# Products with v, of the whole rows and of the next scores stand in one run on TensorE

## The chip, the cores and the metric

The kernel runs on one core of one Trainium2 chip. Its time is the device time of one execution in microseconds (us); the median of three executions before the change is 774.03 us (773.8 to 777.21).

## What is computed

Block-sparse attention, and behind it a feed-forward block without a bias. Batch 4, 8 heads, 768 positions, 64 values per head, blocks of 32 positions (24 blocks):

```
scores = scale * np.matmul(q, k.transpose(0, 1, 3, 2))
mask = |blk_i - blk_j| <= 1, or blk_i or blk_j is the first or the last block,
       or blk_j is one of 3 sampled blocks of blk_i
attn = softmax of scores where mask holds
attn_out = np.matmul(attn, v)
x = attn_out as 3072 tokens x 512
h = np.maximum(x @ w_in, 0.0)        # 512 x 2048
return (h * h @ w_out)               # 2048 x 512
```

Rows of the first and the last block see all keys (the whole rows); every other row sees two edge blocks, three sampled ones and a window of three.

## The kernel before, in words

**Feed-forward part.** The 3072 tokens go in 8 chunks of 384 (`UC` = 3 tiles of 128). `moe(c)` first turns the chunk's x on TensorE (tiles xt), and then, for each of 16 slices f of the hidden layer, issues `project(c, f - 2)` and `hidden(c, f)`. Both split fp32 into a high and a low fp32r part: `hidden` is 12 matmuls of 384 columns into one PSUM bank ph (L754), `project` three groups of 3 matmuls of 512 columns into po_0 to po_2 (L792). Between them ScalarE writes r (L758) and gh (L765), VectorE gf (L770) and the high parts of the weights (L720), GpSimd the low parts (L721, L772).

**Attention part.** The work of the 24 tiles of 128 rows is done in halves of 4 heads: class `Half`, 48 in all. A half does its scores s (64 small matmuls counted as the trace counts them, 64 rows by 32 columns of the array each, L365), maxima and the subtraction on VectorE (L376, L382), 16 exponentials on ScalarE that write straight into turned blocks (L404), a transposition on VectorE (pT, L409), products with v (pv: 64 small matmuls of 128 rows by 32 columns, L450) and the division by the sum on VectorE (`norm`, L465 to L470). After `norm` it loads the v of the next tile's same half: `loads(2)`, 1 or more window loads and 12 sampled ones on SP's queue (L297, L310), into the only buffer that there is for it. Class `Whole` does two heads of a batch's whole rows (4 units a batch): scores g (L528), maxima, exponentials pg, transpositions ptg on TensorE, copies pTg, products with v (pvg: 48 small matmuls, L570) and `norm` (L581 to L589). The unit with pr = 1 loads the batch's second vn behind its products (L215), into the buffer that they read.

**What sets the order.** Each engine runs its instructions in the order in which the program issues them. `moe(c)` is a generator that yields after every third of `hidden` and every group of `project`: six yields for each f, 96 a chunk. At every yield `Stream.step` first resumes the running units whose time has come, in the order in which they began, and then begins new ones. Halves begin every `STEP` = 16 yields, wholes of an even chunk `STEP // 2` = 8 yields behind their half. Inside a unit, `yield lag[...]` says how many yields later it goes on, at least one. With `LAG`, a half's products come 31 yields after its scores, one before the scores of the next half but one; a whole's come 15 yields after its beginning, 23 after the half that it stands beside. `LAG_1` is used for the units of chunk 1, `LAG_0` for those of chunk 0; these units run in their older form, with transpositions on TensorE where `moved` is false.

**Buffers.** s, g, pt, ptg, pv, pvg, xt and ph share 5 PSUM banks (pool `ps`, tag "s"). p, pm and pg share 3 buffers, pT and pTg 2.

## Time and profile before

| | us |
|---|---|
| median of three executions | 774.03 |
| lowest, highest | 773.8, 777.21 |
| the profiled execution | 776.91 |
| its span, first to last instruction | 775.1 |
| PE busy | 748.6 (97%) |
| ACT busy | 498.7 (64%) |
| DVE busy | 494.2 (64%) |
| POOL busy | 474.8 (61%) |

PE is TensorE, DVE VectorE, ACT ScalarE, POOL GpSimd, SP the engine that issues most transfers. In a timeline a row is a run of equal instructions: its start, how long it lasts from the first start to the last end, engine, line, what it writes and reads, and the count; "[... <-X]" would say that the engine stood idle before it, and for what. The time that a run takes of the engine is the distance from its start to the start of the next row, since matmuls overlap at their ends. The trace counts every small fp32 matmul twice (64 for the 32 of a pv).

### The profile page before, as it was taken

The numbers are of one execution on the slowest core, as the hardware profiler recorded it, in microseconds if no ns is written. First come the engines' busy times: TensorE is split into PE (matmuls) and PEld (weight loads), VectorE is DVE, ScalarE is ACT, GpSimd is POOL, SyncE is SP. The second block draws the span as 40 slices with busy tenths as digits, with TensorE's granted clock in tenths as the row PEclk, the third lists the DMA queues.
The fourth block names the chain that finished last, engine by engine and source line by source line (L and its number), as shares of the span: only waits on it lengthen the run. The fifth ranks groups of instructions, "written<-read, shape, count | busy, mean of one in ns | idle before, by whom it ended". The sixth has DMA issues, their size and how long they took to land.

```text
span 775.1 us, 26234 instructions
## 1 busy us (share of the span) xinstructions
PE 748.6 (97%) x9904; PEld 618.2 (80%) x9904; DVE 494.2 (64%) x1005; ACT 498.7 (64%) x1079; POOL 474.8 (61%) x552
## 2 busy tenths in 40 slices
PE   6679998999999999999999999999999999999997
PEld 3556676668888888888888888888888888888996
DVE  5996785657675666667666576667766565644442
ACT  2487877787666776776767767767666685733222
POOL 6993843215567476645556566754556665776885
PEclk9899999999999999999999999999999999999999
DMA  8766789545323535645324343644423342201001
GB/s 277 215 175 207 223 273 329 149 107 164 102 59 100 147 89 151 182 114 147 108 74 110 92 124 104 222 116 140 116 75 98 86 137 74 54 2 42 0 1 41
DMA packets 92289, 97.45 MB, mean 126 GB/s; under 512 B 14787, under 2 KB 79428, under 8 KB 92164
## 3 DMA queue, kind: packets, MB, share of 16 engines
q1 hardware_dynamic: 86036, 72.41, 34.0%
q0 software_dynamic: 5696, 22.58, 8.5%
q8 instruction: 79, 1.29, 0.7%
q10 hardware_dynamic: 432, 0.79, 0.3%
q14 instruction: 46, 0.38, 0.2%
HBM read 89.43 MB, written 6.29 MB: 123 GB/s over the span
## 4 chain that ended last, share of the span: by engine, by line
PE 88%; DVE 4%; DMA 4%; SPq 1%; ACT 1%; issue 1%; ACTq 0%; POOL 0%; POOLq 0%
PE ph L754 34%; PE po L792 31%; PE s L365 6%; PE pv L450 6%; PE po L782 3%; PE g L528 3%; DMA V<-in_v_dram 3%; PE pvg L570 2%; PE xt L739 1%; PE ptg L550 1%; DVE m L376 1%; DVE V L210 1%; DMA KG<-in_k_dram 1%; PE pt L428 1%; DMA kn<-in_kn_dram 1%
## 5 line engine op out<-in xcount | busy, mean ns | idle before, releaser
L404 ACT ACTIVATE pm<-p 32x256 f32<-32x256 f32 x576 | 239.0, 415 | 14.1 <-DVE p L382 5.8
L754 PE MATMUL ph<-xh,wi 128*128 128x384 f32 x832 | 238.9, 348 | 0.0
L792 PE MATMUL po<-wo,gh 128*128 128x512 f32 x672 | 216.1, 403 | 0.0
L772 POOL TENSOR_TENSOR gl<-gf,gh 128x384 fp32r<-128x384 f32 x112 | 115.9, 1035 | 126.3 <-DVE gf L770 110.8
L721 POOL TENSOR_TENSOR wi<-W,wi 128x512 fp32r<-128x512 f32 x104 | 143.4, 1378 | 78.0 <-DVE wi L720 46.4
L758 ACT ACTIVATE r<-ph 128x384 f32<-128x384 f32 x128 | 62.9, 492 | 199.0 <-PE ph L754 198.7
L721 POOL TENSOR_TENSOR wo<-WO,wo 128x512 fp32r<-128x512 f32 x112 | 145.7, 1301 | 56.5 <-DVE wo L720 55.4
L770 DVE SCALAR_TENSOR_TENSOR gf<-ph,r 128x384 f32<-128x384 f32 x112 | 62.3, 557 | 178.1 <-ACT r L758 163.4
L754 PEld LDWEIGHTS ph<-xh,wi 128*128 128x128 f32 x832 | 151.8, 189 | 12.2 <-issue 8.4
L754 PE MATMUL ph<-xl,wi 128*128 128x384 f32 x416 | 143.0, 344 | 0.0
L792 PEld LDWEIGHTS po<-wo,gh 128*128 128x128 f32 x672 | 121.7, 188 | 23.7 <-issue 2.8
L792 PE MATMUL po<-wo,gl 128*128 128x512 f32 x336 | 133.1, 396 | 0.0
L720 DVE CAST wo<-WO 128x512 fp32r<-128x512 f32 x112 | 87.9, 785 | 0.2
L754 PEld LDWEIGHTS ph<-xl,wi 128*128 128x128 f32 x416 | 78.6, 189 | 8.1 <-issue 2.6
L792 PEld LDWEIGHTS po<-wo,gl 128*128 128x128 f32 x336 | 63.2, 188 | 15.5 <-POOL gl L772 0.6
L376 DVE TENSOR_REDUCE m<-s 128x2 f32<-128x512 f32 x96 | 61.7, 684 | 18.0 <-PE s L365 17.6
L765 ACT ACTIVATE gh<-r 128x384 fp32r<-128x384 f32 x112 | 58.9, 526 | 10.1
L450 PEld LDWEIGHTS pv<-V,pT 128*32 128x32 f32 x3072 | 48.0, 109 | 19.7 <-issue 9.2
L450 PE MATMUL pv<-V,pT 128*32 128x65 f32 x3072 | 56.6, 221 | 6.4 <-DMA V<-in_v_dram 2.4
L754 PE MATMUL ph<-xh,WI 128*128 128x384 f32 x192 | 55.2, 348 | 0.8 <-ACT xh L742 0.8
L365 PE MATMUL s<-KG,q 64*32 64x160 f32 x1536 | 50.2, 304 | 0.9 <-issue 0.7
L409 DVE STREAM_TRANSPOSE pT<-pm 128x1024 f32<-128x1024 f32 x36 | 44.6, 1239 | 5.0 <-ACT pm L404 5.0
(81 smaller groups left out, 870.6 us busy)
## 6 DMA issues: line engine op xcount, KB each, us to landing
craw<-in_w_dram POOLq DMA_DIRECT2D x32, 512.0 KB, 5.6
V<-in_v_dram SPq DMA_DIRECT2D x504, 32.5 KB, 1.7
KG<-in_k_dram SPq DMA_DIRECT2D x216, 64.0 KB, 1.9
V<-in_v_dram SPq DMA_DIRECT2D x28, 390.0 KB, 4.1
q<-in_q_dram SPq DMA_DIRECT2D x24, 256.0 KB, 2.9
out_dram<-ot SPq DMA_DIRECT2D x21, 256.0 KB, 2.7
V<-in_v_dram SPq DMA_DIRECT2D x16, 292.5 KB, 4.1
vn<-in_vn_dram SPq DMA_DIRECT2D x5, 780.0 KB, 5.8
```

What stands on the lines that cost most here:

```text
L365: nc.tensor.matmul(self.sb[e][j * BLK : (j + 1) * BLK, i * NSLOT + a : i * NSLOT + z], q[r, j, pr, :], k, start=True, stop=True,)
L376: nc.vector.tensor_reduce(m[:, e], self.sb[e].rearrange("p (i c) -> p i c", i=2), axis=AX, op=ALU.max)
L404: nc.scalar.activation(p[a * BLK : (a + 1) * BLK, j], x[j * BLK : (j + 1) * BLK, :, a], AF.Exp, scale=SCALE)
L450: nc.tensor.matmul(po[j * BLK : (j + 1) * BLK, h * VW : (h + 1) * VW], self.pT[:, j, 2 * e + i, c], v[:, self.u, j, hv : hv + VW], start=( ...
L720: nc.vector.tensor_copy(w[:, 0], src)
L721: nc.gpsimd.tensor_tensor(w[:, 1], src, w[:, 0], op=ALU.subtract)
L754: nc.tensor.matmul(ph[:, :TOK], w, x, start=(i == 0), stop=(i == len(steps) - 1))
L758: nc.scalar.activation(r, ph[:, :TOK], AF.Relu)
L765: nc.scalar.activation(gh, r, AF.Square)
L770: nc.vector.scalar_tensor_tensor(gf, ph[:, :TOK], 0.0, r, op0=ALU.max, op1=ALU.mult)
L772: nc.gpsimd.tensor_tensor(gl, gf, gh, op=ALU.subtract)
L792: nc.tensor.matmul(acc[c][u], g[:, at], w[:, k], start=(f == 0 and i == 0), stop=(f == NF - 1 and i == 2))
```

## The change

The numbers in `LAG` are new, a second test lets `norm` follow its products at once, and the wholes begin 9 yields behind a half in place of 8. A half's products now come 32 yields after its scores and a whole's 32 after those of its half: at the same yield as the scores of the next half but one, and in front of them, since running units are resumed before new ones begin. `LAG_1` sets the old values back for chunk 1.

```diff
-LAG = {"s": 0, "e": 4, "v": 10, "x": 4, "t": 4, "c": 0, "v0": 5, "n": 0}
+LAG = {"s": 0, "e": 4, "v": 11, "x": 4, "t": 4, "c": 0, "v0": 13, "n": -1}
+
+G_AT = 9
 
-LAG_1 = {**LAG, "x": 3, "t": 6}
+LAG_1 = {**LAG, "v": 10, "x": 3, "t": 6, "v0": 5, "n": 0}
...
             po = self.values(bank)
-            yield lag["n"]
+            if lag["n"] >= 0:
+                yield lag["n"]
             self.norm(po)
...
-        both += [(at + i * STEP + STEP // 2, u) for i, u in enumerate(wholes)]
+        both += [(at + i * STEP + G_AT, u) for i, u in enumerate(wholes)]
```

On TensorE, in batch 1 (names are name, batch, tile or pair of heads, half): pv1_0_1 are the products of half 1 of tile 0, pvg1_1 those of the second whole, s1_1_1 the scores two halves on. Before:

```order
L754 MATMUL ph1_2_3424<-xh1_3147,wi1_2_3353 128x384 x2
L570 MATMUL pvg1_1_3429<-vn1_0_2394,pTg1_1_3384 32x65 x24
L754 MATMUL ph1_2_3424<-xl1_3148,wi1_2_3353 128x384
...
L754 MATMUL ph1_3_3506<-xh1_3147,wi1_3_3400 128x384
L450 MATMUL pv1_0_1_3533<-V0_75,pT1_0_1_3413 32x65 x4
...
L792 MATMUL po1_0_3403<-wo1_2_3421,gh1_2_3479 128x512 x2
L792 MATMUL po1_0_3403<-wo1_2_3421,gl1_2_3483 128x512
L365 MATMUL s1_1_1_0_3617<-kn1_1_2598,q1_1_2600 32x96
...
L792 MATMUL po1_1_3404<-wo1_2_3421,gh1_2_3479 128x512 x2
```

And now:

```order
L758 MATMUL ph1_3_3472<-xh1_3122,wi1_3_3400 128x384
L796 MATMUL po1_0_3403<-wo1_2_3421,gh1_2_3441 128x512 x2
L796 MATMUL po1_0_3403<-wo1_2_3421,gl1_2_3445 128x512
L453 MATMUL pv1_0_1_3506<-V0_75,pT1_0_1_3413 32x65 x4
...
L574 MATMUL pvg1_1_3582<-vn1_0_2394,pTg1_1_3397 32x65 x24
L368 MATMUL s1_1_1_0_3617<-kn1_1_2598,q1_1_2600 32x96
...
L796 MATMUL po1_1_3404<-wo1_2_3421,gh1_2_3441 128x512 x2
```

The three small runs, which large matmuls parted, stand together between two groups of `project`. Behind the opening stage, 34 runs of pv are followed by s at once, or by pvg and then s (12 of the 34); before none of them was. The two last halves have no later scores and stand alone as before.

On VectorE, at the same place (rec and recg are the reciprocals in `norm` of a half and of a whole, m the maxima of the scores). Before:

```order
L581 TENSOR_SCALAR recg1_1_3461<-pvg1_1_3429 128x1
L582 RECIPROCAL recg1_1_3461<-recg1_1_3461 128x1
L589 TENSOR_TENSOR x1_0_3174<-pvg1_1_3429,recg1_1_3461 32x64 x2
...
L770 SCALAR_TENSOR_TENSOR gf1_3_3529<-ph1_3_3506,r1_3_3525 128x384
L720 CAST wi1_5_3567<-W15_83 128x512
L465 TENSOR_SCALAR rec1_0_1_3573<-pv1_0_1_3533 128x4
...
L376 TENSOR_REDUCE m1_1_1_3702<-s1_1_1_0_3617 128x2
```

And now:

```order
L774 SCALAR_TENSOR_TENSOR gf1_3_3495<-ph1_3_3472,r1_3_3491 128x384
L724 CAST wi1_5_3500<-W15_83 128x512
L468 TENSOR_SCALAR rec1_0_1_3539<-pv1_0_1_3506 128x4
...
L585 TENSOR_SCALAR recg1_1_3609<-pvg1_1_3582 128x1
L586 RECIPROCAL recg1_1_3609<-recg1_1_3609 128x1
L593 TENSOR_TENSOR x1_0_3241<-pvg1_1_3582,recg1_1_3609 32x64 x2
...
L379 TENSOR_REDUCE m1_1_1_3694<-s1_1_1_0_3617 128x2
```

Both divisions now stand in front of the maxima of the new scores; before, the whole's stood one slice of the hidden layer earlier. On SP's queue the load of the second vn of batches 1 to 3 moves behind the 13 loads of v that follow the half's products; before it stood in front of them.

## Rows read from the trace of the kernel before

**Rows 1.** The page: busy time of TensorE; the chain that ended last.

```profile
PE 748.6 (97%) x9904; PEld 618.2 (80%) x9904; DVE 494.2 (64%) x1005; ACT 498.7 (64%) x1079; POOL 474.8 (61%) x552
...
PE 88%; DVE 4%; DMA 4%; SPq 1%; ACT 1%; issue 1%; ACTq 0%; POOL 0%; POOLq 0%
```

**Rows 2.** Busy time by stretch: length, each engine (instructions), clock, DMA share, GB/s.

```profile
257.00:345.00 88.00, 88.00 (x1185) 75.44 (x1185) 56.73 (x106) 63.54 (x143) 56.07 (x47) 1.00 0.50 139
```

**Rows 3.** Timeline of TensorE, 305 to 315 us: start, length, instruction.

```profile
305.81 1.12 PE L450 MATMUL pv<-V,pT 128*32 128x65 f32 x64
306.86 0.73 PE L792 MATMUL po<-wo,gh 128*128 128x512 f32 x2
...
307.75 0.40 PE L365 MATMUL s<-kn,q 64*32 64x96 f32 x16
...
308.89 0.44 PE L754 MATMUL ph<-xh,wi 128*128 128x384 f32 x1
...
311.08 0.62 PE L792 MATMUL po<-wo,gh 128*128 128x512 f32 x2
...
313.18 0.34 PE L754 MATMUL ph<-xh,wi 128*128 128x384 f32 x1
...
315.26 0.62 PE L792 MATMUL po<-wo,gh 128*128 128x512 f32 x2
```

**Rows 4.** Timeline of TensorE, 334 to 337 us.

```profile
335.59 0.45 PE L754 MATMUL ph<-xl,wi 128*128 128x384 f32 x1
...
336.50 0.40 PE L365 MATMUL s<-kn,q 64*32 64x96 f32 x16
```

**Rows 5.** Timeline of TensorE, 360 to 364 us.

```profile
360.84 0.34 PE L754 MATMUL ph<-xh,wi 128*128 128x384 f32 x1
...
361.63 0.89 PE L570 MATMUL pvg<-vn,pTg 128*32 128x65 f32 x48
362.45 0.44 PE L754 MATMUL ph<-xl,wi 128*128 128x384 f32 x1
...
363.25 1.45 PE L528 MATMUL g<-kn,QG 128*128 128x512 f32 x4
```

**Rows 6.** Timeline of TensorE in the opening stage, 20 to 49 us.

```profile
20.79 0.40 PE L365 MATMUL s<-kn,q 64*32 64x96 f32 x16
...
21.93 0.87 PE L550 MATMUL ptg<-ident,pg 128*128 128x128 f32 x6
...
47.63 1.12 PE L450 MATMUL pv<-V,pT 128*32 128x65 f32 x64 [1.20 <-DVE x L470]
48.68 0.40 PE L365 MATMUL s<-kn,q 64*32 64x96 f32 x16
```

**Rows 7.** The page, costliest groups: busy and mean ns of one.

```profile
L450 PE MATMUL pv<-V,pT 128*32 128x65 f32 x3072 | 56.6, 221 | 6.4 <-DMA V<-in_v_dram 2.4
```

**Rows 8.** Timeline of VectorE, 363 to 374 us.

```profile
363.73 0.14 DVE L581 TENSOR_SCALAR recg<-pvg 128x1 f32<-128x1 f32 x1
...
364.10 0.92 DVE L589 TENSOR_TENSOR x<-pvg,recg 32x64 f32<-32x64 f32 x4
...
372.28 0.15 DVE L465 TENSOR_SCALAR rec<-pv 128x4 f32<-128x4 f32 x1
...
373.57 1.29 DVE L376 TENSOR_REDUCE m<-s 128x2 f32<-128x512 f32 x2
```

**Rows 9.** Timeline of TensorE, two pv that follow each other, and an s.

```profile
369.52 1.12 PE L450 MATMUL pv<-V,pT 128*32 128x65 f32 x64
...
371.46 0.40 PE L365 MATMUL s<-kn,q 64*32 64x96 f32 x16
...
386.22 1.12 PE L450 MATMUL pv<-V,pT 128*32 128x65 f32 x64
```

**Rows 10.** Timeline of SP's queue: the first transfer behind the v loads.

```profile
379.20 0.37 SPq L235 DMA_DIRECT2D q<-in_q_dram  x1
```

**Rows 11.** The loads of vn on SP (line 215): time to landing.

```profile
DMA to landing us min/median/max: 4.1/5.8/7.8
```

## The prediction

> **What bounds the kernel now.** I read the page first, then the busy times by stretch, then the timeline of TensorE run by run, and last VectorE and SP's queue at the places where instructions move. The page says that TensorE is busy for 97% of the span and that 88% of the chain that ended last is TensorE [rows 1]. In the stretch from 257 to 345 us it is busy for all 88 us at the granted clock 1.00, while VectorE, ScalarE and GpSimd are busy for 56 to 64 us of it [rows 2]. So a shorter time has to come out of TensorE itself: fewer instructions, or the same ones with less lost between them. The change takes no instruction away, so only what is lost between them is left. For that the reader is to look at the timeline in another way: not at how long a row lasts, but at the distance to the next row's start, and to compare equal runs with different neighbours.

> **What a small run costs its neighbours.** Nine po take 2.10 us (311.08 to 313.18), that is 0.70 for three, and twelve ph take 2.08 us (313.18 to 315.26), that is 0.69 for four [rows 3]. Three po between a pv and an s take 0.89 us (306.86 to 307.75) [rows 3]: 0.19 more. Four ph between a pv and an s take 0.91 us (335.59 to 336.50) [rows 4]: by the rounded rows 0.22 more, and 0.21 is what I take. Four ph in front of a pvg take 0.79 us (360.84 to 361.63) and four behind it 0.80 us (362.45 to 363.25) [rows 5]: 0.10 for going in and 0.11 for coming out. So each passage from large matmuls to small ones and back costs about 0.2 us of TensorE, and it is booked in the large runs.

> **The change part by part.**

> First, pv in front of s. In 34 places a run of three po (17 times) or of four ph (17 times) stood between them and now does not. What is lost in that run goes: 17 times 0.19 and 17 times 0.21 make 6.8 us. Whether the new neighbours lose something between them is seen in the opening stage, where they already stood together. A pv in front of an s takes 1.05 us (47.63 to 48.68) [rows 6], and one in front of a po takes 1.05 us as well (305.81 to 306.86) [rows 3]. An s behind a pvg takes 1.14 us (20.79 to 21.93) [rows 6], and one between large runs 1.14 us (307.75 to 308.89) [rows 3]. So nothing is added, and the 6.8 us stand whole. All of it lies on the path, since TensorE has no idle time here.

> Second, the 12 pvg. Each was a passage of its own, in and out, and now stands inside one that is there anyway: 12 times 0.21 is 2.5 us. In three places an xt follows the pvg before; I take the same price there.

> Third, pv in front of pvg. A pv's last matmul starts at 305.81 + 1.12 - 0.22 (the mean of one [rows 7]) = 306.71, and the po behind it at 306.86 [rows 3]: 0.15 us go by, where the 63 steps inside the run take 0.90 us, 0.014 each. No row shows a pv followed by a pvg. It can't cost more than this 0.15, which other successors pay, nor less than 0.014. The row nearest to it is the inside of pv's own run, since a pvg has the same shape (128 rows by 32 columns, 65 values). I take that: 12 times 0.135 is 1.6 us, and zero as the other end.

> [...]

> Fourth, what else moves. The g and ptg of the wholes stand one yield later, still between large runs, and I cost them at nothing. The divisions of halves and wholes now run on VectorE while TensorE works on pvg, s and the next large runs; that work is the cover, and what it costs if the cover is too thin is the last rival below. The products wait longer for their turn, so pT and pTg are ready earlier relative to use; nothing waits there. On SP the second vn of batches 1 to 3 goes behind 13 loads of v: a rival too, and nothing in the sum. The loads of v for the next tile start with the end of pv as before. Behind the vn on SP are q and the keys of the tile after the next, which are not due for two halves.

> The sum is 6.8 + 2.5 + 1.6 = 10.9 us, with 9.3 us as the end without the third term. Against the profiled execution: the span 775.1 becomes 764.2 us, and with the 1.8 us outside the span its 776.91 becomes 766.0. That execution stands 2.9 us above the median of the runs, 774.03; the same 10.9 us off the median give 763.1 us, which is the forecast.

> **The rivals.**

> Every change of shape costs the same. A pv is 128 rows by 32 columns, an s 64 by 32, so pv to s is a change too. If each change has one price, half of the 0.2, then a half had four changes and now has three: 34 times 0.1 make 3.4 us, and with the wholes' 2.5 and 1.6 the sum is 7.5 us: 766.5 us. [...] Against it: rows 6, where pv and s side by side take what they take apart. For it: those are a few places in a stage with waits.

> A vn that comes late. The loads of v behind a pv keep SP busy until 379.20 where the pv began at 369.52 [rows 9, 10]: 9.7 us. A vn then lands 4.1 to 7.8 us later [rows 11], 13.8 to 17.5 us behind the start of the pv. The pvg that reads it follows the next pv, which before begins 16.7 us behind the first [rows 9]; less some 0.5 us for what is saved, and with the 0.9 us that pv itself now puts in front of the pvg, it is due at about 17.1 us. At the median there are 1.6 us to spare; at the slowest landing it is 0.4 us late. In three places that is 1.2 us, and with 2 us more of contention at each 7 us: 764 to 770 us.

> Nothing comes of it. The 0.2 us at the boundaries only moves: the long run of small matmuls (176 as the trace counts them, where 128 is the most that stood together) is fed more slowly than the short ones, so that each group gives back what it saved. Then the time is 771 to 774. For it: no row shows such a run. Against it: pv and s, 128 together, lose nothing [rows 6].

> VectorE becomes what TensorE waits for. A half's division takes 1.29 us up to the maxima (372.28 to 373.57), and a whole's 1.29 us (363.73 to 364.10 and 0.92 more) [rows 8]. Both now stand in front of the maxima of the new s, and the two banks of s come free only behind maxima and subtraction. Five banks serve all; when those of s come late, the hidden run two further on has none and TensorE stops. A wait of 0.65 us, half a division, in each of the 34 groups would be 22 us, and the time 785. It decides from 0.32 us a group on (10.9 / 34): above that the change is slower than before. For it: the work stands closer together than ever. Against it: the maxima began 0.97 us behind the end of s before as well (that s began at 371.46 [rows 9] and takes 1.14 us, so it ended at 372.60), because the division stood in front of them there too; the pvg and s themselves, 0.8 and 1.1 us, cover most of the two divisions; and VectorE was idle for a third of the stretch [rows 2].

> **How the numbers follow.** The forecast with its own spread (with or without the third term, and up to 1.5 us for things that I left out) 0.70, 761.5 to 765.5 us. Every change at one price 0.10, 766.5. A late vn 0.07, 764 to 770. Nothing 0.08, 771 to 774. VectorE 0.05, from 774 up. What a measurement of this kernel can tell from no change is about 0.5%, 3.9 us: faster means below 770.2, slower above 777.9. Faster: 0.70 + 0.10 + 0.07 and a little of the others, 0.88. Within: 0.08. Slower: 0.04. The range that should hold 8 in 10 is 760.8 to 767.5 us: the likeliest case, the one price, and half of the late vn.

> **What would show it.** In the profile after, a pv in front of a pvg should take 0.91 us, one in front of an s 1.05, a pvg in front of an s 0.82, and s 1.14. Three po between two large runs should take 0.70 where they took 0.89, and only the first large run behind an s should still carry about 0.11. VectorE's maxima should begin within 1.2 us of the end of s, and no ph or ptg should show idle time on TensorE. The first step is wrong if s behind pv or pvg takes over 1.2 us or pv in front of s over 1.1; the third, if pv in front of pvg takes 1.05. If a third whole of batches 1 to 3 shows a wait for vn, that rival has come. The prediction as a whole is wrong if the busy share of TensorE falls, that is, if it has begun to wait.

## The result and the profile after

The changed kernel takes 767.28 us (median of 6 executions, 764.2 to 770.41), the kernel before beside it on the same chip 774.4 us. The ratio is 0.9898 with a 95% interval of 0.9868 to 0.9929: faster by 1.0%. The forecast of 763.1 us is 4.2 us too low, and the measured time stands at the upper end of the range, 760.8 to 767.5 us. Measured again later (e6), the same program had a median of 765.55 us against 775.74 for the kernel before, a ratio of 0.9891 (0.9844 to 0.9937). The profiled execution of the change took 766.68 us, its span 764.9.

On the page, TensorE is busy for 11 us less than before, and its share falls from 97 to 96% [rows 1]. The forecast had named a falling share as the sign that TensorE has begun to wait; the sign came, by a little: TensorE is not busy for 27.3 us of the span where it was 26.5.

```profile
PE 737.6 (96%) x9904; PEld 619.8 (81%) x9904; DVE 497.8 (65%) x1005; ACT 499.3 (65%) x1079; POOL 477.0 (62%) x552
...
PE 86%; DVE 5%; DMA 4%; issue 1%; SPq 1%; ACT 1%; ACTq 0%; POOL 0%; POOLq 0%
```

The timeline of TensorE after, from 303.61 us, answers to [rows 3]: a half's products and scores between two large runs.

```profile
303.61 0.63 PE L796 MATMUL po<-wo,gh 128*128 128x512 f32 x2
...
304.40 1.12 PE L453 MATMUL pv<-V,pT 128*32 128x65 f32 x64
305.45 0.40 PE L368 MATMUL s<-kn,q 64*32 64x96 f32 x16
...
306.59 0.44 PE L758 MATMUL ph<-xh,wi 128*128 128x384 f32 x1
...
308.77 0.62 PE L796 MATMUL po<-wo,gh 128*128 128x512 f32 x2
...
310.87 0.34 PE L758 MATMUL ph<-xh,wi 128*128 128x384 f32 x1
```

Read the distances from start to start: pv 1.05 us, s 1.14, as forecast. The twelve ph behind s take 2.18 us where twelve took 2.08 [rows 3]: they still pay 0.10 for coming out. The three po in front of pv take 0.79 us (303.61 to 304.40) where nine between large runs take 2.10, 0.70 for three: they pay 0.09 for going in. So one passage of about 0.2 us is left for each group; the forecast's list of signs named only the run behind s.

Where a whole stands between (it answers to [rows 5]), and the first ptg behind it:

```profile
349.59 1.12 PE L453 MATMUL pv<-V,pT 128*32 128x65 f32 x64
350.53 0.86 PE L574 MATMUL pvg<-vn,pTg 128*32 128x65 f32 x48
351.32 0.40 PE L368 MATMUL s<-kn,q 64*32 64x96 f32 x16
...
352.46 0.44 PE L758 MATMUL ph<-xh,wi 128*128 128x384 f32 x1
...
353.96 0.82 PE L554 MATMUL ptg<-ident,pg 128*128 128x128 f32 x6
354.53 0.60 PE L758 MATMUL ph<-xh,wi 128*128 128x384 f32 x2
```

A pv in front of a pvg takes 0.94 us here by the rounded rows, the pvg in front of s 0.79, s 1.14. The forecast was 0.91, 0.82 and 1.14.

What nobody had booked is seen, behind the opening stage, only in batch 1, from 170 to 224 us. The same group at 186.92 us, timeline of TensorE after:

```profile
186.92 1.12 PE L453 MATMUL pv<-V,pT 128*32 128x65 f32 x64
187.86 0.86 PE L574 MATMUL pvg<-vn,pTg 128*32 128x65 f32 x48
188.65 0.40 PE L368 MATMUL s<-kn,q 64*32 64x96 f32 x16
188.84 0.48 PE L368 MATMUL s<-KG,q 64*32 64x160 f32 x16
189.11 0.35 PE L368 MATMUL s<-kn,q 64*32 64x96 f32 x10
190.42 0.28 PE L368 MATMUL s<-kn,q 64*32 64x96 f32 x3 [0.95 <-issue]
...
190.98 0.73 PE L796 MATMUL po<-wo,gh 128*128 128x512 f32 x2
```

In the middle of the scores TensorE stops for 0.95 us, and the releaser is "issue": it waits for no other engine and no transfer of data that the profile shows. From 188.65 to 190.98 the scores take 2.33 us in place of 1.14. The waits of TensorE from 170 us to the end are one line after (columns: line, releaser, us in total, times, longest), and none before:

```profile
PE s L368 <- issue: 2.2, 2, 1.3
```

By distances there are four such places in batch 1: the scores at 172.27, 188.65 and 206.04 us took 0.22, 1.19 and 1.68 us over 1.14, and the ph behind the fourth group 0.23 us over its usual length. That is 3.3 us.

**Where the 10.2 us of span went.** The first scores of batch 1 begin at 137.85 us before and at 135.67 after. So 2.2 us lie in the opening stage, whose order the change leaves alone. From there to the end it is 637.3 us before and 629.2 after: 8.0 us. With the 3.3 us of new waits put back, the change saved 11.3 to 11.4 us of TensorE's time there, against a sum of 10.9.

The 2.2 us of the opening come mostly from a transfer that lands at another time, and from the clock behind it. Timeline of TensorE before, a pv that waits for the v of its tile:

```profile
129.88 0.31 PE L450 MATMUL pv<-V,pT 128*32 128x65 f32 x6
131.00 0.32 PE L450 MATMUL pv<-V,pT 128*32 128x65 f32 x8 [0.81 <-DMA V<-in_v_dram]
132.89 0.98 PE L450 MATMUL pv<-V,pT 128*32 128x65 f32 x50 [1.57 <-DMA V<-in_v_dram]
```

and after:

```profile
130.81 0.31 PE L453 MATMUL pv<-V,pT 128*32 128x65 f32 x6
131.51 0.32 PE L453 MATMUL pv<-V,pT 128*32 128x65 f32 x8 [0.39 <-DMA V<-in_v_dram]
132.31 0.98 PE L453 MATMUL pv<-V,pT 128*32 128x65 f32 x50 [0.48 <-DMA V<-in_v_dram]
```

The pv takes 3.9 us before and 2.4 after, 1.5 less. Behind it, before, the granted clock is 0.50 from 134.04 to 137.45 us, and the large matmuls from the end of this pv to the first scores of batch 1 take 4.05 us; after, the clock stays at 1.00 there and they take 2.45, 1.6 less. Ahead of this pv the change is 0.9 us later, which leaves 2.2. The same pv took 1.05, 1.55 and 6.93 us in other executions below, so much of the spread of the times comes from here. That is why the experiments are read in the stretch from batch 1's first scores to the end, beside the times.

### The profile page after: what moved, and what is told of

It is laid out like the page before. It is cut to its first block, busy times and chain, and to the rows that moved or that the text cites. A ratio compares the mean times of both kernels' runs of the same rounds, so it can differ in the third digit from the quotient of the medians.

```text
span 764.9 us, 26233 instructions
## 1 busy us (share of the span) xinstructions
PE 737.6 (96%) x9904; PEld 619.8 (81%) x9904; DVE 497.8 (65%) x1005; ACT 499.3 (65%) x1079; POOL 477.0 (62%) x552
## 3 DMA queue, kind: packets, MB, share of 16 engines
q8 instruction: 79, 1.29, 0.7%
## 4 chain that ended last, share of the span: by engine, by line
PE 86%; DVE 5%; DMA 4%; issue 1%; SPq 1%; ACT 1%; ACTq 0%; POOL 0%; POOLq 0%
PE ph L758 34%; PE po L796 31%; PE s L368 6%; PE pv L453 6%; PE po L786 3%; DMA V<-in_v_dram 3%; PE g L532 3%; PE pvg L574 1%; PE xt L743 1%; PE ptg L554 1%; DVE V L212 1%; DVE m L379 1%; DMA KG<-in_k_dram 1%; DMA kn<-in_kn_dram 1%; SPq L312 1%
## 5 line engine op out<-in xcount | busy, mean ns | idle before, releaser
L796 PE MATMUL po<-wo,gh 128*128 128x512 f32 x672 | 213.8, 399 | 0.0
L796 PEld LDWEIGHTS po<-wo,gh 128*128 128x128 f32 x672 | 123.4, 188 | 22.3 <-issue 2.8
L724 DVE CAST wo<-WO 128x512 fp32r<-128x512 f32 x112 | 82.9, 740 | 0.0
L385 DVE TENSOR_TENSOR p<-s,m 128x512 f32<-128x512 f32 x72 | 46.1, 681 | 2.4 <-PE ptg L554 2.2
```

The costliest lines, as they stand in the source:

```text
L724: nc.vector.tensor_copy(w[:, 0], src)
L796: nc.tensor.matmul(acc[c][u], g[:, at], w[:, k], start=(f == 0 and i == 0), stop=(f == NF - 1 and i == 2))
```

## The theory and its rival

The theory: TensorE's instructions arrive in blocks, and a long run of small matmuls uses them up faster than the next block comes. The page's queues after have the line (queue, kind: packets, MB, share of the DMA engines):

```profile
q8 instruction: 79, 1.29, 0.7%
```

79 packets with 1.29 MB are 16.3 KB each (16,384 bytes in the packets' own records). The page counts 9904 matmuls and as many weight loads, and the trace holds 412 other instructions of TensorE, 20,220 in all: 256 for each packet. A group of pv, pvg and s is 352 instructions in 2.9 us, so 256 of them last 2.1 us; a pv and an s alone are 256, in 2.2 us. In the two groups with the longest waits such a packet starts at 188.11 and 205.79 us, during the pvg, and takes 1.0 and 1.2 us; TensorE goes on 2.3 and 2.6 us behind its start (read from the packets' own records). If the theory holds, the wait depends on where in a group the blocks of 256 fall, and on nothing else of the program. Numbering TensorE's instructions in the trace from the first, as I did for the expectations, blocks begin 100, 116, 136 and 167 instructions behind the start of batch 1's four groups, 193, 210, 230 and 5 in batch 2, 31, 48, 68 and 99 in batch 3.

The rival: batch 1 is the place where keys, v or vn come late, and "issue" hides a transfer; then the waits stay in batch 1 whatever stands in front.

## The experiments

The kernel before, measured beside e1, e2, e3 and e5, had a median of 775.06 us; beside e4, e6 and e7 it had 775.74. "The stretch" is the time from batch 1's first scores to the end of the profiled execution.

**e1: halves only.** The products of the halves stand in front of the scores, those of the wholes apart from both.

```diff
-LAG = {"s": 0, "e": 4, "v": 11, "x": 4, "t": 4, "c": 0, "v0": 13, "n": -1}
+LAG = {"s": 0, "e": 4, "v": 11, "x": 4, "t": 4, "c": 0, "v0": 5, "n": -1}
-G_AT = 9
+G_AT = 8
```

> The halves alone: a half's products and the scores of the next half but one stand together (34 places, 256 TensorE instructions in a run), the wholes' products go back between large matmuls. Theory (two boundaries of 0.1 us go at each place, and the waits inside s in batch 1 come from TensorE's instruction blocks running out in runs of 352 instructions): 6.8 us less TensorE time behind 160 us than before, no idle time of 0.2 us or more inside an s behind 160 us, some 767 to 768 us. Rival (s stops in batch 1 because its keys or a bank come late, whatever stands in front of it): the s in batch 1, near 190 and 207 us, still stop for about 1 us each, and the time is 769 to 771.

Measured: 768.34 us, ratio 0.9911 (0.9876 to 0.9947); the stretch 629.9 us, 7.4 less than before, and no wait of TensorE behind 170 us. The first term alone was 6.8. The 0.6 over it are in three ptg between two ph: each took about 0.2 us less, in this kernel as in the change (353.96 to 354.53 above, 0.57 us; 0.80 before). Its 34 runs of 256 instructions in 2.2 us show no wait, and nothing is late in batch 1 here, though keys and v are used at the same places.

**e2: wholes only.** The products of the wholes stand behind those of the halves, and large matmuls, 3 po or 4 ph, stand between them and the scores as before.

```diff
-LAG = {"s": 0, "e": 4, "v": 11, "x": 4, "t": 4, "c": 0, "v0": 13, "n": -1}
+LAG = {"s": 0, "e": 4, "v": 10, "x": 4, "t": 4, "c": 0, "v0": 13, "n": -1}
-G_AT = 9
+G_AT = 8
```

> The wholes alone: a half's products and the whole's products stand together (12 places, 224 instructions), the scores stand apart as before. Theory: 12 passages of 0.21 us and 12 times 0.12 to 0.14 us between pv and pvg go, 4.0 to 4.2 us, some 770 us; no idle time inside an s behind 160 us. Rival (each change of shape has one price, so that the scores' side gains less and the wholes' side more than was booked): more than 5 us here and less than 5 us where the halves alone stand together.

Measured: 774.12 us, ratio 0.9992 (0.9964 to 1.002); the stretch 635.1 us, only 2.2 less than before. The expectation that no wait stands inside s was wrong. Timeline of TensorE in e2:

```profile
171.10 0.62 PE L758 MATMUL ph<-xh,WI 128*128 128x384 f32 x2
171.56 0.34 PE L758 MATMUL ph<-xl,WI 128*128 128x384 f32 x1
171.73 0.34 PE L758 MATMUL ph<-xh,WI 128*128 128x384 f32 x1
172.00 0.40 PE L368 MATMUL s<-kn,q 64*32 64x96 f32 x16
172.19 0.48 PE L368 MATMUL s<-KG,q 64*32 64x160 f32 x16
172.46 0.32 PE L368 MATMUL s<-kn,q 64*32 64x96 f32 x2
174.01 0.31 PE L368 MATMUL s<-kn,q 64*32 64x96 f32 x7 [1.23 <-issue]
```

Three runs of scores of batch 1 lost 2.4 us (1.47, 0.69, 0.24). Four ph are 0.9 us but only 8 instructions, so for the supply the group stays one long dense run, which the expectation had overlooked. Without these waits the gain is 4.6 us: the second and third terms, 4.1, and the same three ptg.

**e3: 100 instructions in front.** The change, and ahead of everything 25 idle products of 128 x 32 that nobody reads (50 matmuls and 50 weight loads as the trace counts).

```diff
+    spare = bank("spare")
+    for _ in range(25):
+        nc.tensor.matmul(spare[:, 0:32], ident, ident[:, 0:32], start=True, stop=True)
```

> The changed kernel with 25 products of the identity with 32 of its columns in front, while TensorE waits for its first data: 100 instructions more in its stream, whose result nobody reads. Theory (blocks of 256 instructions): all later block boundaries come 100 instructions earlier in the program. In batch 1's runs of pv, pvg and s they then stand at about 0, 16, 36 and 67 instead of 100, 116, 136 and 167, and in batch 2's at about 93, 110, 130 and 161 instead of 193 to 261: the idle time inside s leaves 170 to 225 us and appears between 345 and 400 us, about 1 us in two or three of the four runs. Batch 3's (187 to 255) stay free. Total within 2 us of the changed kernel. Rival (data late in batch 1, or the transfers of that stretch): the idle time stays near 190 and 207 us and none appears near 350 to 400 us.

Measured: 774.07 us, ratio 0.9963 (0.9937 to 0.9988). The total missed what was expected, since the opening got 8 us longer: the idle products ran until 13.75 us where the first g began at 6.6. But the waits moved as the theory says. Batch 1, with blocks at 0, 16, 36 and 67, lost nothing. Batch 2, free in the change, now has them, here the group with the block at 110 by my count:

```profile
370.86 1.12 PE L453 MATMUL pv<-V,pT 128*32 128x65 f32 x64
371.79 0.86 PE L574 MATMUL pvg<-vn,pTg 128*32 128x65 f32 x48
372.59 0.40 PE L368 MATMUL s<-kn,q 64*32 64x96 f32 x16
372.78 0.48 PE L368 MATMUL s<-KG,q 64*32 64x160 f32 x16
373.05 0.34 PE L368 MATMUL s<-kn,q 64*32 64x96 f32 x7
374.81 0.29 PE L368 MATMUL s<-kn,q 64*32 64x96 f32 x5 [1.43 <-issue]
```

**e4: 200 in front.** The same with 50 idle products.

```diff
+    spare = bank("spare")
+    for _ in range(50):
+        nc.tensor.matmul(spare[:, 0:32], ident, ident[:, 0:32], start=True, stop=True)
```

> The change with 50 idle products of 128x32 (100 instructions on TensorE with their weight loads) put in front, where e3 had 25 (50 products and loads, counted with their splits as 100): the whole instruction stream of TensorE is shifted by 200 against the change. Theory of the instruction blocks (256 instructions each; a group pv, pvg, s stalls when a block begins about 100 to 155 instructions behind its start): the blocks then begin 156 and more behind the start of batch 1's groups, below 61 in batch 2's, and 87, 104, 124 and 155 behind the start of batch 3's. So the waits of 1 to 2 us inside the scores leave batches 1 and 2 and stand in batch 3, at 104 and 124 surely, at 87 and 155 perhaps: 2 to 3 us in all. Theory of the keys or of data that come late: the waits stay in batch 1 at the same three scores, whatever stands in front, 3.1 us. Theory of chance: they are found at other places than these. The opening gets longer by the idle products, so the total says nothing here: what is read is where the waits are, and their sum.

Measured once: 783.56 us, most of it the longer opening. Batch 2 has no wait, batch 3 has two, and one stands at the first group of batch 1. The waits of TensorE from 530 us to the end:

```profile
PE s L368 <- issue: 2.3, 2, 1.3
```

They stand where blocks begin at 124 and 155 by my count (1.56 and 1.46 us by distances); 104 lost only 0.13 and 87 nothing. The group of batch 1 at 156 lost 1.96 us, where I had expected none; the other three, at 172, 192 and 223, lost nothing. So the window reached further up than I had said, and began later.

**Where exactly TensorE stops.** Over the four profiles with groups of pv, pvg and s in all batches (the change, e3, e4, and the change again, e6) and e2 there are 12 waits of 0.4 us or more at "issue" behind 170 us. The last instruction before each has these numbers, counted from TensorE's first in the trace, which is 0: 5568 and 6080 in the change, the same two in e6, 5056 and 5568 in e2, 10688, 11200 and 11712 in e3, 5312, 16320 and 16832 in e4. Every one of them is a multiple of 256 plus 192. So the blocks are there, and their true boundary lies 192 behind the one of my count (64 instructions in front of the first record would explain it; that was not tested). With the boundary put right, these are the groups of the change, e6, e3 and e4 in which it falls 279 to 364 instructions behind the start (the group ends at 352; lost: us over the usual length):

| boundary (by my count) | kernel, batch | lost in the group | in the large run behind |
|---|---|---|---|
| 279 (87) | e4, 3 | 0 | 0 |
| 285 (93) | e3, 2 | 0 | 0 |
| 291 (99) | change, 3; e6 | 0; 0 | 0 |
| 292 (100) | change, 1; e6 | 0.22; 0 | 0 |
| 296 (104) | e4, 3 | 0.13 | 0 |
| 302 (110) | e3, 2 | 1.66 | 0 |
| 308 (116) | change, 1; e6 | 1.19; 1.43 | 0 |
| 316 (124) | e4, 3 | 1.56 | 0 |
| 322 (130) | e3, 2 | 1.17 | 0 |
| 328 (136) | change, 1; e6 | 1.68; 1.11 | 0 |
| 347 (155) | e4, 3 | 1.46 | 0 |
| 348 (156) | e4, 1 | 1.96 | 0 |
| 353 (161) | e3, 2 | 0 | 1.0 |
| 359 (167) | change, 1; e6 | 0 | 0.23; 0.25 |
| 364 (172) | e4, 1 | 0 | 0 |

With three different shifts the waits follow the boundary and not the batch. In these rows a wait of 1 us or more needs a boundary 302 or more instructions behind the group's start. That 256 small products and loads lie in front of it is not enough, since from 279 to 296 they do too. At 353 the group is just over, and the large run behind it waits. The rival of late data falls.

The packets' own records tell the rows apart. In all seven cases from 279 to 296 the last packet in front of the boundary starts before the group, by 0.0 to 1.0 us; in all from 302 on it starts 1.0 to 1.9 us behind the group's start. Wherever TensorE lost 0.13 us or more in a group, it went on 2.3 to 2.9 us behind the start of that packet. So a wait goes with a packet that starts only inside the dense run. That this packet carries the next block is inferred from one packet for each block.

**e5: batch 1 apart.** The change, but the wholes of chunk 2, those of batch 1, keep their products away from the halves' as in e1.

```diff
+LAG_2 = {**LAG, "v0": 5}
...
-        both += [(at + i * STEP + G_AT, u) for i, u in enumerate(wholes)]
+        both += [(at + i * STEP + (8 if c == 2 else G_AT), u) for i, u in enumerate(wholes)]
...
-            work.add(at, c, lambda u=u, lag=LAG_1 if c == 1 else LAG: u.run(bank, lag))
+            work.add(at, c, lambda u=u, lag={1: LAG_1, 2: LAG_2}.get(c, LAG): u.run(bank, lag))
```

> The changed kernel, but the wholes of batch 1 alone stand apart from the halves as before, so that no run of 352 instructions is left there. Theory: the waits inside s near 190 and 207 us go (3.1 us), four passages come back (4 times 0.34, 1.4 us): 1.7 us less than the changed kernel. Rival (data late): the waits stay and the time is 1.4 us above the changed kernel.

Measured: 765.55 us, ratio 0.9889 (0.9852 to 0.9925); the stretch 627.7 us, 1.5 less than in the change. The waits inside s are gone. From 170 us on one wait of TensorE is left, and it is the late vn:

```profile
PE pvg L575 <- DMA vn<-in_vn_dram: 0.4, 1, 0.4
```

The arithmetic closes: 3.3 us of waits gone, four passages (4 x 0.21) and four pv in front of pvg (4 x 0.14) given back, and 0.4 for vn leave 1.5.

**e6 and e7: the change and e5 again, beside each other.** No edit against the change and against e5.

> The changed kernel itself once more, to stand beside e7 on the same chip. Instruction blocks: the three waits stand at the same three scores of batch 1 (1.36, 2.33 and 2.81 us for a run of 16 x 64 scores that takes 1.14 elsewhere), since the program is the same, within 0.2 us each; time 764 to 770 us. Chance in the fetching: the waits differ from the first profile in place or size by more than 0.5 us.

> The change with the products of the whole rows kept apart from the half tiles in batch 1 alone (e5 again), beside the change on the same chip. Instruction blocks: no wait inside the scores, the stretch from the first scores of batch 1 to the end 1.5 to 1.7 us shorter than in e6, and the median of the times 1 to 2 us below e6's if the opening falls alike in both; rival: the difference of e5 was the opening's spread, and the medians lie within 0.5 us.

Measured: e6 765.55 us, ratio 0.9891 (0.9844 to 0.9937); e7 763.8 us, ratio 0.9841 (0.9809 to 0.9872), the lowest time of all kernels here. In e6 the waits stand at the same places as in the first profile but differ by 0.2 to 0.6 us in size. That is more than the 0.2 expected, and the largest difference passes the 0.5 us set as the sign of chance in the fetching. One of them:

```profile
189.11 0.35 PE L368 MATMUL s<-kn,q 64*32 64x96 f32 x10
```

in the change became in e6

```profile
187.19 0.35 PE L368 MATMUL s<-kn,q 64*32 64x96 f32 x10
188.73 0.28 PE L368 MATMUL s<-kn,q 64*32 64x96 f32 x3 [1.19 <-issue]
```

The wait comes behind the same tenth matmul of that row, 1.19 us long in place of 0.95. So the program sets the place, and something that differs between executions the size. It goes with the packet: the one for this wait starts 0.16 us later behind its group's start in e6 and the wait is 0.24 longer; for the next group's wait it starts 0.51 us earlier and the wait is 0.57 shorter. Why a packet starts earlier or later was not tested. In e7 there is no wait of TensorE behind 170 us, vn included. The stretch is 627.2 us against 629.0 in e6, 1.8 less (1.5 to 1.7 expected). But 0.4 of it is a wait that has nothing to do with the order: in e6 the first scores of batch 1 take 1.52 us, because ScalarE copies their keys late (KG, L279). That leaves 1.4, as the waits of e6, 2.8, less the 1.4 given back would make it. The medians differ by 1.75 us, though their intervals overlap: that e7 beats the kernel before is shown, that it beats the change is shown by the stretch in two pairs of profiles (1.5 and 1.4 us) and only likely by the times.

With the waits taken out, the stretch is the same in all kernels with the whole change:

| profile | stretch, us | waits in it | without them |
|---|---|---|---|
| the change | 629.2 | 3.3 | 625.9 |
| e6, the change again | 629.0 | 2.8, and 0.4 for the copied keys | 625.8 |
| e3 | 629.8 | 3.8 | 626.0 |
| e4 | 631.4 | 5.1, and 0.3 for the copied keys | 626.0 |

Before, it is 637.3 us with no wait. So the regrouping is worth 11.4 us, and the supply of instructions takes 2.8 to 5.1 us of it back, depending on where the blocks fall.

## Why the prediction was right, and where it was off

*What bounds the kernel.* Right: with TensorE's losses between runs gone, the time fell, and no other engine took its place.

*First, pv in front of s: 6.8 us.* Right in mechanism and size. Behind 160 us, three po between a pv and an s took 0.893 us (median of 17) and four ph 0.901 (17); three po between large runs take 0.698 after. In 22 places pv in front of s takes 1.05 us and s 1.14, as it took between large runs, and e1 alone gave 7.4 with the ptg.

*Second, the passages of the wholes: 2.5 us.* Right: entering cost 0.09 us and leaving 0.11, 12 times 0.21.

*Third, pv in front of pvg: 1.6 us.* Right: 0.932 us in place of 1.046 (12 places), and the pvg behind it 0.794 in place of 0.818; together 12 x 0.138 = 1.7. The upper end of the bounds was the true one.

*Fourth, the rest at nothing.* Off by 0.6 us in the change's favour: the three ptg between two ph. The timeline before shows what they waited for (PEld is TensorE's weight load):

```profile
356.10 0.86 DVE L470 TENSOR_TENSOR x<-pv,rec 32x256 f32<-32x256 f32 x2
...
356.47 1.04 PE L550 MATMUL ptg<-ident,pg 128*128 128x128 f32 x6
...
357.07 0.20 PEld L550 LDWEIGHTS ptg<-ident,pg 128*128 128x128 f32 x2 [0.24 <-PE ptg L550]
...
357.27 0.42 PE L754 MATMUL ph<-xl,wi 128*128 128x384 f32 x1
```

The view names the ptg itself. But the last two of its six matmuls stand behind a wait for a semaphore that VectorE raised last at 356.97, at the end of a half's division (x), and the same holds at the other two. After, that division ends at 352.49, and the ptg begins at 353.96. So "TensorE has no idle time here" was not quite so: a thin wait for `norm` was there, and the change took it away.

*"So nothing is added, and the 6.8 us stand whole."* This is the sentence that failed, in three of the 12 groups with a whole and in the run behind a fourth. It was drawn from runs of at most 128 matmuls; the 176 of a group with pvg are 352 instructions, more than one block of 256. And in one of the opening's runs of 128, at 31.99 us, the trace before shows a wait: 1.33 us at "issue" inside the s, until 35.57 us, 2.5 us behind the start of a packet at 33.08; rows 6 show only the run at 47.63. The named sign, an s over 1.2 us, came: 1.36, 2.33 and 2.81 us; so did the sign for the whole, a falling busy share. This was the mechanism of the rival "nothing comes of it", at 0.08, which I had drawn as all or nothing. It is neither: in the groups of the table it costs 1 to 2 us where a block of instructions ends 302 to 353 instructions behind a group's start, and 0.25 us or less elsewhere. By the row "q8 instruction" and the group's length this could have been asked before.

*The other rivals.* "Every change of shape one price" is out: pv to s costs nothing over pv to po. The late vn did not come in the change; e5 shows 0.4 us of it once, e7 none. VectorE made TensorE wait nowhere behind 170 us. My sign for it was badly chosen, though. VectorE's timeline after, behind the scores that end at 352.46:

```profile
351.23 0.15 DVE L468 TENSOR_SCALAR rec<-pv 128x4 f32<-128x4 f32 x1
...
352.52 0.16 DVE L585 TENSOR_SCALAR recg<-pvg 128x1 f32<-128x1 f32 x1
...
353.86 0.43 DVE L724 CAST wi<-W 128x512 fp32r<-128x512 f32 x1
354.21 0.42 DVE L724 CAST wo<-WO 128x512 fp32r<-128x512 f32 x1
354.66 1.29 DVE L379 TENSOR_REDUCE m<-s 128x2 f32<-128x512 f32 x2
```

The maxima begin 2.2 us behind the scores, not within 1.2; two casts stand in front of them besides the divisions. Before, they began up to 2.1 us behind as well, and the five banks carried that.

*The sum and the time.* The sum of 10.9 was 11.4 on the chip; the 3.3 us of waits make it 8.0, and that is the error of the forecast that is explained: 3 of the 4.2 us. The rest is within the spread of the opening, which moved by 2 us between two profiles and by more in others. That the time still lies inside the range, by 0.2 us, is luck: its upper end was drawn for the one price and the late vn, and neither came.

## What to carry to other kernels

A passage from large matmuls to small ones and back costs TensorE about 0.2 us here, so small runs belong together, and equal shapes next to each other: a pv took 0.932 us in front of a pvg and 1.046 in front of a large matmul. But count instructions and not only time: where small matmuls and weight loads follow each other as densely as here, 352 in 2.9 us, ask for the page's instruction queue and where its blocks fall; a wait called "issue" in the middle of a run was its sign, and 100 or 200 instructions at the very front moved it to another batch (e3, e4). Such a loss is a lottery that an experiment with another order can win by luck: read the waits apart from what the order itself gives.
